# Adding u to the stored MLP output in DRAM, with accumulating transfers, in place of identity products on TensorE

## The chip, the cores and the metric

The kernel runs on one core of one Trainium2 chip. The metric is the device time of one execution in microseconds, as the median of several runs. A core has five engines with a queue of instructions each: TensorE (PE, with its weight loads as PEld), VectorE (DVE), ScalarE (ACT), GpSimd (POOL) and SyncE (SP), which issues most of the transfers. Transfers between DRAM and the on-chip memory run on 16 DMA engines.

## The reference

Causal block attention, then a token mix and an MLP with a residual, then a gated convolution:

```python
# attention: B=8, H=8, S=576, D=64; blocks of 64, block i sees blocks j <= i
attn = softmax(where(mask, q @ k^T / sqrt(D), -1e9));  x = attn @ v      # (8, 576, 512)
h = x^T @ U @ V                  # U 576x32, V 32x576, along the tokens
u = x + h^T
x = u + relu(u @ w_ch1) @ w_ch2  # 512 -> 2048 -> 512
gate = sigmoid(causal conv of 5 taps over the tokens, per channel)
out = (gate * (x @ w_val)) @ w_out
```

The change touches the `u +` of the MLP's output and nothing else of what is computed.

## The kernel before

Products run in float32r on operands split in a high and a low part (`hi_act`, L90, on ACT; `lo`, L96, on DVE or POOL), and each product is three: high by high, low by high, high by low. The 4608 tokens of all batches make 9 groups of 512 (`NG`, `GS`); features stand on partitions, so that a tile of u is 128 features by 512 tokens, and d counts the four feature blocks. The 2048 hidden features make 16 blocks f (`NF`), so the MLP runs in 144 steps s, step s being f = s mod 16 of group g = s // 16.

`mix_H` (L820) forms u: a product in PSUM, an add on DVE that leaves u in `xt` (L835), its high part `uh` on ACT (L836), its low part `ul` on POOL (L837). A batch has 576 tokens, so its u is cut in pieces for two groups or three, and pieces for a group too far ahead wait in the list `later` until the group two before has had its last hidden block (`y_done`).

`emit_h1(s)` makes a hidden block: 12 products (L963) into PSUM, relu to `hh` on ACT (L991), the low part `hl` on DVE (L992). `emit_o(s)` multiplies it with w2: 12 products (L1015) into four PSUM banks `acc`, one for each d, that collect over the 16 blocks of a group. `emit_o` runs one step behind `emit_h1`. At f = 0 it takes fresh banks, and the four d get eight products with an identity matrix `identr` first, one with `uh` and one with `ul` (L1008): this is how u comes into the sum. At f = 15 ACT copies the four banks to `y` (L1027) and SP writes each to DRAM, `y_s[g]` (L1028). From the first group to the seventh the pool of `y` has two buffers, so the third copy waits until the first write has landed and the fourth for the second.

Around a group boundary PE's order is: the w2 products of f = 15 of the old group, hidden blocks f = 0 and f = 1 of the new one, the identity products, the w2 products of f = 0. Boundary n below is the one at which group n begins, n from 0 to 8. Between the parts `gap` puts pieces of the attention of a later batch, a fixed pace of them for each group; attention ends during group 6, and group 7's part of u with it.

The order on PE is as the program is written. On the other engines the program's scheduler sets it, from a timeline that it estimates; instructions under `high_priority` go ahead. SP issues the loads of w2 (L951, 512 KB for each step), of q, k and v (L334, L345) and the writes of `y_s`, one after the other, and waits in its queue where a buffer isn't free. POOL does low parts, among them `vlo` of the attention (L97), which PE's pPV products use. The last stage reads `y_s` back (`load_y`, L1067): groups 0 and 1 during group 8, the rest after the MLP.

Of the kernel before, what the change touches and what calls it, by code (L numbers as in the profile page):

```python
# [8 lines left out]
F32 = mybir.dt.float32  # L9
F32R = mybir.dt.float32r  # L10
# [3 lines left out]
ALU = mybir.AluOpType  # L14
# [3 lines left out]
P = 128  # L18
# [4 lines left out]
def attn_moe_gate_kernel(ctx: ExitStack, tc: tile.TileContext, q, k, v, U, V, w1, w2, wval, convw, wout, out):  # L23
# [8 lines left out]
    ND = DM // P  # L32
    NF = DFF // P
    NP = H // 2
    GS = 512
    groups = [(t, min(GS, NT - t)) for t in range(0, NT, GS)]
    NG = len(groups)
# [41 lines left out]
    PAT = (0,1)  # L79
    URG = True  # L80
    UVAT = 14
    LOW = 2000
    NB32 = S // 32

# [3 lines left out]
    vec, act, pool, pe, sp = nc.vector, nc.scalar, nc.gpsimd, nc.tensor, nc.sync  # L88

    def hi_act(o, i):  # L90
        act.copy(o, i)  # L91
# [4 lines left out]
    def lo(eng, o, i, h):  # L96
        eng.tensor_tensor(o, i, f32(h), op=ALU.subtract)  # L97
# [50 lines left out]
    dram = ctx.enter_context(tc.tile_pool(name="dram", bufs=1, space=DRAM))  # L148
    const = ctx.enter_context(tc.tile_pool(name="const", bufs=1, side="left"))
# [13 lines left out]
    def open_mlp_psum():  # L163
        first.close()
        psum["acc"] = mlp.enter_context(tc.tile_pool(name="accp", bufs=1, space=PSUM, side="left"))
# [36 lines left out]
    ps_p = att.enter_context(tc.tile_pool(name="psp", bufs=ABUF, space=PSUM, side="right"))  # L202

    y_s = [dram.tile([P, ND, n], F32, name=f"y_s{g}") for g, (_, n) in enumerate(groups)]
    w2_s = [dram.tile([P, 2, DM], F32, name=f"w2_s{f}") for f in range(NF)]

    def ypos(t):
# [12 lines left out]
    ident = ac_p.tile([P, P], F32, name="ident")  # L220
# [6 lines left out]
        pool.memset(both[64 * a:64 * a + 64, 64 * a:64 * a + 64], 1.0)  # L227
    unit = const.tile([KC, KC], F32, name="unit")
    pool.tensor_copy(unit, ident[0:KC, 0:KC])
    identr = const.tile([P, P], F32R, name="identr")  # L230
    pool.tensor_copy(identr, ident)

    w1hi = w1_p.tile([P, ND, DFF], F32R, name="w1hi")
    w1lo = w1_p.tile([P, ND, DFF], F32R, name="w1lo")
# [26 lines left out]
    def setup_uv():  # L261
        ur = fetch(U, NTT * R, [(slice(0, n), slice(i * R, i * R + R), slice(t0, t0 + n), slice(0, R)) for i, (t0, n) in enumerate(tok)], True)
        ur = ur.rearrange("p (i r) -> p i r", r=R)
        for c in (0, 2, 3):
            (hi_act if UVE else hi_vec)(ust1[:, :, c * R:(c + 1) * R], ur)
        lo(vec, ust1[:, :, R:2 * R], ur, ust1[:, :, 0:R])
        for h in range(2):
            hs = slice(h * HS, (h + 1) * HS)
            vr = fetch(V, HS, [(slice(c * R, c * R + R), slice(0, HS), slice(0, R), hs) for c in range(4)])
            (hi_act if UVE else hi_vec)(vst[:, hs], vr)  # L270
            lo(vec, vst[3 * R:4 * R, hs], vr[3 * R:4 * R, :], vst[3 * R:4 * R, hs])
# [485 lines left out]
    ut = {}  # L757
    gst = {}

    def u_tiles(g):  # L760
        if g not in ut:
            ut[g] = [u_p.tile([P, ND, GS], F32R, tag="u" + x, name="u" + x) for x in "hl"]
        return ut[g]


    def mix_pieces(b):
        t0, t1 = b * S, (b + 1) * S
        r = []
        for g, (a, n) in enumerate(groups):
            lo_t, hi_t = max(a, t0), min(a + n, t1)  # L770
            if lo_t < hi_t:
                r.append((g, lo_t - t0, hi_t - t0, lo_t - a))
        return r
# [3 lines left out]
    def mix_H2(pn):  # L777
        mix_H(pn, 0)
        yield
        mix_H(pn, 1)  # L780
# [39 lines left out]
    def mix_H(pn, i):  # L820
        pcs = mix_pieces(pn // NP)
        if i >= len(pcs):
            return
        gi, a0, a1, off = pcs[i]
        if gi >= 2 and gi > y_done[0] + 2:
            later.append((pn, i))
            return
        xt = xts[pn]
        d = pn % NP
        uh, ul = u_tiles(gi)  # L830
        w = a1 - a0
        ps = ps_p.tile([P, 512], F32, tag="a", name="pH")
        pe.matmul(ps[:, 0:w], gst[pn], vst[:, a0:a1], start=True, stop=True)
        with tc.high_priority():
            vec.tensor_tensor(xt[:, a0:a1], ps[:, 0:w], xt[:, a0:a1], op=ALU.add)  # L835
        hi_act(uh[:, d, off:off + w], xt[:, a0:a1])  # L836
        lo(pool, ul[:, d, off:off + w], xt[:, a0:a1], uh[:, d, off:off + w])  # L837

# [116 lines left out]
    accs = {}  # L955
# [20 lines left out]
    def emit_h1(s, gap):  # L976
# [19 lines left out]
        gap()  # L996
        hts[s] = (hh, hl)

    def emit_o(s, gap):
        g, f = divmod(s, NF)  # L1000
        t0, n = groups[g]
        if f == 0:
            if g == 0:
                open_mlp_psum()
            accs[g] = [psum["acc"].tile([P, GS], F32, tag=f"acc{d}", name=f"acc{d}") for d in range(ND)]
            for d in range(ND):
                for i, u in enumerate(ut[g]):
                    pe.matmul(accs[g][d][:, 0:n], identr, u[:, d, 0:n], start=(i == 0), stop=False)  # L1008
        acc = accs[g]
        hh, hl = hts.pop(s)  # L1010
        w = w2t.pop(s)
        for d in range(ND):
            ds = slice(d * P, (d + 1) * P)
            for i, (wi, x) in enumerate(((0, hh), (0, hl), (1, hh))):
                pe.matmul(acc[d][:, 0:n], w[:, wi, ds], x[:, 0:n], start=False, stop=(f == NF - 1 and i == 2))  # L1015
            if d == 1:
                gap()
        gap()
        if f == NF - 1:
            ut.pop(g)  # L1020
            for d in range(ND):
                if pbp and g < NG - 1:
                    y = pbp["g"].tile([P, GS + HALO], F32, tag="gt", name="gt")
                else:
                    y = late["y"].tile([P, GS], F32, tag="y", name="y")
                with tc.high_priority():
                    act.copy(y[:, 0:n], acc[d][:, 0:n])  # L1027
                sp.dma_start(out=y_s[g][:, d, :], in_=y[:, 0:n])  # L1028
# [42 lines left out]
    def split_tiles(g, pb):  # L1071
        gate[g][1:3] = [pb.tile([P, ND, GS], F32R, tag="y" + x, name="y" + x) for x in "hl"]
# [19 lines left out]
    def val_begin(g, pg):  # L1092
        gated[g] = [pg.tile([P, ND, GS], F32R, tag="g" + x, name="g" + x) for x in "hl"]

    def emit_val(g, e, pg, pvs):
        t0, n = groups[g]
        y, yh, yl, gt, segs, wd = gate[g]
        gh, gl = gated[g]
        vh, vl = wv["v"]
        es = slice(e * P, (e + 1) * P)  # L1100
        ps = pvs.tile([P, GS], F32, tag="val", name="val")
        i = 0
        for d in range(ND):
            for w, x in ((vh, yh), (vh, yl), (vl, yh)):
                pe.matmul(ps[:, 0:n], w[:, d, es], x[:, d, 0:n], start=(i == 0), stop=(i == 3 * ND - 1))  # L1105
                i += 1
        gf = pg.tile([P, GS], F32, tag="gf", name="gf")
        for o, m, pp in segs:
            latest[0] = vec.tensor_tensor(gf[:, o:o + m], ps[:, o:o + m], gt[e][:, pp - HALO:pp - HALO + m], op=ALU.mult)
        hi_act(gh[:, e, 0:n], gf[:, 0:n])  # L1110
        lo(vec, gl[:, e, 0:n], gf[:, 0:n], gh[:, e, 0:n])
# [56 lines left out]
    for i, done in enumerate(stream):  # L1168
        if i == UVAT:
            setup_uv()  # L1170
# [14 lines left out]
    def gap():  # L1185
        tick_count[0] += 1
        if tick_count[0] % EVERY == 0:
            flush_later()
        pace[0] += pace[1]
        while pace[0] > 0 and pace[2] == 0:  # L1190
            pace[0] -= 1.0
            r = next(stream, 2)
            if r:
                pace[2] = r
                if r == 2:
                    while later:
                        flush_later()
                    open_pb()

    gated_conv[0] = GATE0  # L1200
    for s in range(NS + LAG):
        g, f = divmod(s, NF)
# [14 lines left out]
        if s < NS:  # L1217
# [11 lines left out]
            if g == NG - 1 and 4 <= f < 4 + 2 * ND:  # L1229
                g_, d = divmod(f - 4, ND)  # L1230
# [6 lines left out]
    with pb1:  # L1237
        with tc.tile_pool(name="pbs2", bufs=1, side="left") as pbs2, \
                tc.tile_pool(name="pbgd", bufs=2, side="left") as pbgd, \
                tc.tile_pool(name="pbo", bufs=3, side="left") as pbo, \  # L1240
                tc.tile_pool(name="pbpo", bufs=3, space=PSUM, side="left") as pbpo:
            pbs = (pbp["y1"], pbs2)
            pbps = pbp["ps"]
            for g in range(NG + 1):
                if g < NG:
                    val_begin(g, pbgd)
                    if g + 1 < NG:
                        split_tiles(g + 1, pbs[(g + 1) % 2])
                    for e in range(ND):
                        emit_val(g, e, pbgd, pbps)  # L1250
                        if g + 1 < NG:
                            split_y(g + 1, e)
                            if g > 0:
                                emit_gate(g + 1, e)
                    gate.pop(g)
                    if g + 2 < NG:
                        load_y(g + 2)
                if g > 0:
                    emit_out(g - 1, pbo, pbpo)
# [30 lines left out]
```

## Time and profile before

| | |
|---|---|
| time, median of 3 runs | 1433.97 us (1433.51 to 1435.35) |
| profiled execution: time, and its span | 1437.6 us, 1435.8 us |
| PE busy | 1392.8 us, 97% of the span |
| DVE busy | 1026.1 us, 71% |
| ACT busy | 698.5 us, 49% |
| POOL busy | 317.9 us, 22% |
| moved by the transfers | 163.58 MB |

The span is from the first to the last instruction that the profiler saw; the time has 1.8 us around it. Busy shares are averages over stages. Matmuls are pipelined: one is shown as 0.39 us long while the next starts 0.23 us after it, so the distance between starts is the price of one.

### The profile page before, as it was taken

Reading aid. Unit: us, or ns where it says so; the run is one execution under the profiler, and the core shown is the slowest. Engines: PE = TensorE matmul, PEld = TensorE weight load, DVE = VectorE, ACT = ScalarE, POOL = GpSimd, SP = SyncE. Lnnn points to the kernel's source line nnn. Section 1 sums busy time; section 2 is a strip of 40 time slices with the busy share of each in tenths; the row PEclk is TensorE's granted clock in tenths of the full one; section 3 lists DMA queues with packets and bytes.
Section 4 is the critical chain, followed back from the end, with each engine's and each line's share of the span. In section 5 each row is a group of like instructions: output and inputs, shape, how many; then the busy total and the mean of one; then the engine's idle time right before and its main releaser. Section 6 shows DMA issues by size and latency. Waiting matters only on the chain.

```text
span 1435.8 us, 20136 instructions
## 1 busy us (share of the span) xinstructions
PE 1392.8 (97%) x6762; PEld 1083.0 (75%) x6762; DVE 1026.1 (71%) x2105; ACT 698.5 (49%) x1539; POOL 317.9 (22%) x467
## 2 busy tenths in 40 slices
PE   6898978999999999999999999999999999999999
PEld 4666656777777777777777777778888888788887
DVE  5987889687777886888687787866225245499991
ACT  5775544555655555546455555555233211344342
POOL 3353441111121121112111211121032000344310
PEclk9999999999999999999999999999999999999999
DMA  6666775433343443434343333332255433223311
GB/s 110 155 156 202 226 235 140 114 84 97 90 113 84 93 106 103 98 87 125 84 99 88 110 88 99 84 97 83 87 177 170 151 104 131 75 83 101 110 52 66
DMA packets 246290, 163.58 MB, mean 114 GB/s; under 512 B 197669, under 2 KB 212261, under 8 KB 246186
## 3 DMA queue, kind: packets, MB, share of 16 engines
q1 hardware_dynamic: 243818, 161.99, 40.3%
q8 instruction: 54, 0.88, 0.3%
q10 hardware_dynamic: 2368, 0.30, 0.2%
q14 instruction: 50, 0.41, 0.1%
HBM read 134.98 MB, written 27.26 MB: 113 GB/s over the span
## 4 chain that ended last, share of the span: by engine, by line
PE 84%; DVE 6%; DMA 5%; ACT 3%; issue 1%; SPq 1%; POOL 0%; ACTq 0%; DVEq 0%; POOLq 0%
PE acc L1015 26%; PE h L963 25%; PE pPV L734 8%; PE o L1129 7%; PE val L1105 7%; PE pS L415 6%; DMA raw<-in_moe_w_ch_dram 3%; PE pG L810 1%; PE acc L1008 1%; PE pS L454 1%; DVE wa L125 1%; DVE wa L143 1%; DMA rawk<-in_k_dram 1%; PE pPV L542 1%; ACT s L469 1%
## 5 line engine op out<-in xcount | busy, mean ns | idle before, releaser
L1015 PE MATMUL acc<-hh,w 128*128 128x512 f32 x1152 | 401.5, 401 | 0.0
L1015 PEld LDWEIGHTS acc<-hh,w 128*128 128x128 f32 x1152 | 216.7, 188 | 65.4 <-issue 21.0
L963 PE MATMUL h<-uh,w1hi 128*128 128x512 f32 x576 | 237.1, 412 | 2.8 <-DVE xt L835 1.0
L963 PE MATMUL h<-uh,w1lo 128*128 128x512 f32 x576 | 226.5, 393 | 0.0
L963 PE MATMUL h<-ul,w1hi 128*128 128x512 f32 x576 | 226.0, 392 | 0.0
L1015 PE MATMUL acc<-hl,w 128*128 128x512 f32 x576 | 225.4, 391 | 0.0
L992 DVE SCALAR_TENSOR_TENSOR hl<-h,hh 128x512 fp32r<-128x512 f32 x144 | 98.5, 684 | 130.4 <-ACT hh L991 129.1
L991 ACT ACTIVATE hh<-h 128x512 fp32r<-128x512 f32 x144 | 85.8, 596 | 174.7 <-PE h L963 168.9
L963 PEld LDWEIGHTS h<-uh,w1hi 128*128 128x128 f32 x576 | 108.8, 189 | 46.6 <-issue 19.5
L97 POOL TENSOR_TENSOR vlo<-vstk,vhi 128x320 fp32r<-128x320 f32 x46 | 42.1, 916 | 457.0 <-ACT vhi L91 415.4
L963 PEld LDWEIGHTS h<-uh,w1lo 128*128 128x128 f32 x576 | 108.5, 188 | 24.2
L1015 PEld LDWEIGHTS acc<-hl,w 128*128 128x128 f32 x576 | 108.5, 188 | 19.5 <-issue 0.7
L963 PEld LDWEIGHTS h<-ul,w1hi 128*128 128x128 f32 x576 | 108.9, 189 | 18.7 <-issue 0.2
L1087 DVE SCALAR_TENSOR_TENSOR gt<-yb,cw,gt 128x516 f32<-128x516 f32 (+1 forms) x144 | 115.2, 831 | 1.4
L415 PE MATMUL pS<-tq,tk 64*128 64x320 f32 (+4 forms) x576 | 97.5, 427 | 5.0 <-ACT za L420 2.2
L97 POOL TENSOR_TENSOR yl<-yb,yh 128x512 fp32r<-128x512 f32 (+7 forms) x64 | 66.8, 1076 | 107.2 <-ACT yh L91 107.1
L420 ACT COPY s<-pS 128x320 f32<-128x320 f32 (+2 forms) x128 | 60.1, 497 | 52.3 <-PE pS L415 51.1
L97 POOL TENSOR_TENSOR ul<-xt,uh 128x512 fp32r<-128x512 f32 (+7 forms) x64 | 56.4, 888 | 93.4 <-ACT uh L91 93.2
L415 PEld LDWEIGHTS pS<-tq,tk 64*128 64x128 f32 x576 | 45.0, 185 | 41.9 <-issue 23.0
L670 ACT ACTIVATE s<-s 128x448 f32<-128x448 f32 (+1 forms) x62 | 43.8, 711 | 62.0 <-DVE s L646 61.8
L646 DVE TENSOR_TENSOR s<-s,mb 128x64 f32<-128x64 f32 (+4 forms) x160 | 67.3, 483 | 0.3
L97 DVE TENSOR_TENSOR el<-s,eh 128x448 fp32r<-128x448 f32 (+1 forms) x62 | 46.7, 787 | 17.6 <-PE pPV L734 9.8
(188 smaller groups left out, 2678.7 us busy)
## 6 DMA issues: line engine op xcount, KB each, us to landing
w<-w_s SPq DMA_DIRECT2D x144, 512.0 KB, 3.3
rawq<-in_q_dram SPq DMA_DIRECT2D x128, 72.0 KB, 2.9
out_dram<-ot SPq DMA_DIRECT2D x35, 256.0 KB, 2.0
rawk<-in_k_dram SPq DMA_DIRECT2D x124, 72.0 KB, 3.1
vstk<-in_v_dram SPq DMA_DIRECT2D x64, 128.0 KB, 2.6
raw<-in_moe_w_ch_dram SPq DMA_DIRECT2D x64, 128.0 KB, 2.8
raw<-in_moe_w_ch_dram SPq DMA_DIRECT2D x16, 512.0 KB, 3.9
w_s<-wo SPq DMA_DIRECT2D x16, 512.0 KB, 3.8
```

Source lines behind the costliest of these rows:

```text
L97: eng.tensor_tensor(o, i, f32(h), op=ALU.subtract)
L415: pe.matmul(t[:, o:o + w], tk[me, kslice(j)], tq[me, a0:a1], start=True, stop=True)
L420: act.copy(stt[n][half_of[j]][:, d:d + o], t[:, 0:o])
L646: noted(3, vec.tensor_tensor(sv(n, j), sv(n, j), mb[:, q0[j]:], op=ALU.subtract))
L734: pe.matmul(o_, l_, r_, start=(i == 0), stop=(i == len(todo) - 1))
L963: pe.matmul(ps[:, 0:n], w[:, d, fs], x[:, d, 0:n], start=(d == 0 and i == 0), stop=(d == ND - 1 and i == 2))
L991: act.activation(hh[:, 0:n], ps[:, 0:n], AF.Relu)
L992: latest[0] = vec.scalar_tensor_tensor(hl[:, 0:n], ps[:, 0:n], 0.0, f32(hh[:, 0:n]), op0=ALU.max, op1=ALU.subtract)
L1015: pe.matmul(acc[d][:, 0:n], w[:, wi, ds], x[:, 0:n], start=False, stop=(f == NF - 1 and i == 2))
L1087: vec.scalar_tensor_tensor(gt[d][:, 0:gw], y[:, d, j:j + gw], cw[:, d, j:j + 1], gt[d][:, 0:gw], op0=ALU.mult, op1=ALU.add)
L1105: pe.matmul(ps[:, 0:n], w[:, d, es], x[:, d, 0:n], start=(i == 0), stop=(i == 3 * ND - 1))
L1129: pe.matmul(ps[:m, cs], x[:, e, a:a + m], w[:, e, cs], start=(i == 0), stop=(i == 3 * ND - 1))
```

## The change

The identity matrix in float32r and the 72 identity products are gone (8 in each of 9 groups); the first w2 product of f = 0 now starts the bank (`start=True`). `mix_H` writes each finished piece of u to DRAM, to a new tile `u_s` in the layout of `y_s` (64 transfers on SP's queue, one for each piece). `add_u(g)` issues four transfers from POOL's queue, from DRAM to DRAM, that add `u_s[g]` to `y_s[g]` where it lies, 256 KB each. It stands in `emit_o` at f = 2 (`UAT`) of the group after; for the last group in the last stage, after the second `emit_val` of group 0.

```diff
@@ mix_H
         with tc.high_priority():
             vec.tensor_tensor(xt[:, a0:a1], ps[:, 0:w], xt[:, a0:a1], op=ALU.add)
+        sp.dma_start(out=u_s[gi][:, d, off:off + w], in_=xt[:, a0:a1])
         hi_act(uh[:, d, off:off + w], xt[:, a0:a1])
@@
+    def add_u(g):
+        for d in range(ND):
+            pool.dma_start(out=y_s[g][:, d, :], in_=u_s[g][:, d, :], accum_op=ALU.add)
+
     def emit_o(s, gap):
...
-            for d in range(ND):
-                for i, u in enumerate(ut[g]):
-                    pe.matmul(accs[g][d][:, 0:n], identr, u[:, d, 0:n], start=(i == 0), stop=False)
         acc = accs[g]
+        if f == UAT and g > 0:
+            add_u(g - 1)
...
-                pe.matmul(acc[d][:, 0:n], w[:, wi, ds], x[:, 0:n], start=False, stop=(f == NF - 1 and i == 2))
+                pe.matmul(acc[d][:, 0:n], w[:, wi, ds], x[:, 0:n], start=(f == 0 and i == 0), stop=(f == NF - 1 and i == 2))
@@ last stage
                         emit_val(g, e, pbgd, pbps)
+                        if g == 0 and e == 1:
+                            add_u(NG - 1)
```

On PE nothing but the 72 products leaves the order. On SP's queue, at boundary 3, before (y_s_115 is the output of group 2, `rawq` and `rawk` are raw tiles of q and k, `w` is a w2 tile):

```order
L951 DMA w_5585<-w_s_137 128x1024
L334 DMA rawq<-in_q_dram 32x18x32 x2
L334 DMA rawk<-in_k_dram 32x18x32 x2
L334 DMA rawq<-in_q_dram 32x18x32 x2
L334 DMA rawk<-in_k_dram 32x18x32 x2
L951 DMA w_5706<-w_s_122 128x1024
L1028 DMA y_s_115<-y 128x512 x2
L951 DMA w_5739<-w_s_123 128x1024
L1028 DMA y_s_115<-y 128x512 x2
```

And now (u_s_125 and u_s_126 belong to groups 3 and 4):

```order
L836 DMA u_s_125<-xt 128x320
L334 DMA rawq<-in_q_dram 32x18x32
L836 DMA u_s_126<-xt 128x256 x2
L334 DMA rawq<-in_q_dram 32x18x32
L836 DMA u_s_126<-xt 128x256
L334 DMA rawk<-in_k_dram 32x18x32
L952 DMA w_5729<-w_s_131 128x1024
L334 DMA rawk<-in_k_dram 32x18x32
L1032 DMA y_s_115<-y 128x512 x2
L836 DMA u_s_126<-xt 128x256
L952 DMA w_5762<-w_s_132 128x1024
L1032 DMA y_s_115<-y 128x512
```

Four pieces of u now stand ahead of the first two writes of `y_s`, and one more ahead of the other two. On ACT's queue at the same place, before (the four copies out of the banks with a high part of u between them; `xt`, `lt`, `eh` and `ef` are attention work):

```order
L1027 COPY y<-acc_4367 128x512
L1027 COPY y<-acc_4368 128x512
L91 CAST uh<-xt 128x256
L1027 COPY y<-acc_4369 128x512
L1027 COPY y<-acc_4370 128x512
L735 COPY xt<-pPV 64x128
L736 COPY lt<-pPV 64x128
L91 CAST eh<-s_5162 128x448
L91 CAST eh<-s_5163 128x768
```

And now:

```order
L1031 COPY y<-acc_4386 128x512
L1031 COPY y<-acc_4387 128x512
L92 CAST uh<-xt 128x256
L1031 COPY y<-acc_4388 128x512
L735 COPY xt<-pPV 64x128
L736 COPY lt<-pPV 64x128
L92 CAST eh<-s_5179 128x448
L1031 COPY y<-acc_4389 128x512
L92 CAST eh<-s_5180 128x768
```

The fourth copy has moved three places back; the third, which waits for the first write of `y_s`, stands where it stood. On POOL's queue the four accumulating transfers stand around a low part of v, here those of boundary 3 as they are now:

```order
L98 TENSOR_TENSOR ul<-xt,uh 128x256 x4
L1002 DMA y_s_115<-u_s_124 128x512 x3
L98 TENSOR_TENSOR vlo<-vstk_166,vhi 128x320
L1002 DMA y_s_115<-u_s_124 128x512
L98 TENSOR_TENSOR vlo<-vstk_165,vhi 128x320
```

Three of the four stand ahead of the first `vlo`; before, no transfer stood on this queue at this place.

## Rows read from the trace of the kernel before

**Rows 1.** Busy time by stretch: window and length in us, then each engine (instructions)

```profile
113.00:263.00 150.00, 131.68 (x633) 96.35 (x630) 124.99 (x241) 75.07 (x164) 48.11 (x54) 0.98 0.64 192
263.00:1149.00 886.00, 883.92 (x4293) 689.90 (x4292) 615.79 (x1357) 449.51 (x941) 157.58 (x265) 1.00 0.39 105
```

**Rows 2.** Instructions of L1008: count, shortest, median, longest ns, first and last start

```profile
L1008 PE MATMUL acc<-uh,identr x36: 387/389/499, 113.3 to 1149.4; 128*128 128x512 f32 x36
```

**Rows 3.** PE in order of time at boundary 3: start us, length us, instruction

```profile
547.24 0.39 PE L1008 MATMUL acc<-uh,identr 128*128 128x512 f32 x1
...
549.06 0.39 PE L1015 MATMUL acc<-hh,w 128*128 128x512 f32 x1
```

**Rows 4.** ACT and DVE in order of time at boundary 3

```profile
541.47 1.07 ACT L1027 COPY y<-acc 128x512 f32<-128x512 f32 x2 [3.00 <-DMA y_s<-y]
...
547.27 0.60 ACT L991 ACTIVATE hh<-h 128x512 fp32r<-128x512 f32 x1
...
547.90 0.69 DVE L992 SCALAR_TENSOR_TENSOR hl<-h,hh 128x512 fp32r<-128x512 f32 x1
```

**Rows 5.** First identity product and hl of f=0, boundaries 1, 2, 4, 5, 6, 7

```profile
276.33 0.47 PE L1008 MATMUL acc<-uh,identr 128*128 128x512 f32 x1
272.16 0.69 DVE L992 SCALAR_TENSOR_TENSOR hl<-h,hh 128x512 fp32r<-128x512 f32 x1 [1.99 <-ACT hh L991]
413.60 0.40 PE L1008 MATMUL acc<-uh,identr 128*128 128x512 f32 x1
413.04 0.69 DVE L992 SCALAR_TENSOR_TENSOR hl<-h,hh 128x512 fp32r<-128x512 f32 x1
680.68 0.39 PE L1008 MATMUL acc<-uh,identr 128*128 128x512 f32 x1
681.43 0.65 DVE L992 SCALAR_TENSOR_TENSOR hl<-h,hh 128x512 fp32r<-128x512 f32 x1
813.64 0.39 PE L1008 MATMUL acc<-uh,identr 128*128 128x512 f32 x1
814.61 0.65 DVE L992 SCALAR_TENSOR_TENSOR hl<-h,hh 128x512 fp32r<-128x512 f32 x1
946.73 0.39 PE L1008 MATMUL acc<-uh,identr 128*128 128x512 f32 x1
948.18 0.65 DVE L992 SCALAR_TENSOR_TENSOR hl<-h,hh 128x512 fp32r<-128x512 f32 x1
1058.64 0.39 PE L1008 MATMUL acc<-uh,identr 128*128 128x512 f32 x1
1058.22 0.69 DVE L992 SCALAR_TENSOR_TENSOR hl<-h,hh 128x512 fp32r<-128x512 f32 x1 [2.81 <-ACT hh L991]
```

**Rows 6.** SP's queue at boundary 3: writes of y_s, two and two

```profile
537.03 1.01 SPq L1028 DMA_DIRECT2D y_s<-y  x2
542.08 1.71 SPq L1028 DMA_DIRECT2D y_s<-y  x2
```

**Rows 7.** Stretches before and during that write: last two columns DMA share, GB/s

```profile
532.00:537.00 5.00, 5.00 (x25) 4.16 (x24) 4.48 (x11) 2.77 (x6) 3.17 (x4) 1.00 0.78 122
537.00:541.50 4.50, 4.50 (x25) 3.81 (x24) 4.25 (x14) 1.03 (x4) 0.80 (x1) 1.00 0.94 298
```

**Rows 8.** POOL's vlo after boundary 3, and the first product that uses it

```profile
546.12 0.89 POOL L97 TENSOR_TENSOR vlo<-vstk,vhi 128x320 fp32r<-128x320 f32 x1 [6.77 <-DMA vstk<-in_v_dram]
...
556.91 0.37 PE L734 MATMUL pPV<-eh,vlo 128*64 128x448 f32 x1
```

**Rows 9.** A w2 load in group 8, its first product, and all such loads (KB, us to landing)

```profile
1152.78 0.32 SPq L951 DMA_DIRECT2D w<-w_s  x1
...
1160.75 0.39 PE L1015 MATMUL acc<-hh,w 128*128 128x512 f32 x1
...
w<-w_s SPq DMA_DIRECT2D x144, 512.0 KB, 3.3
```

More of the change, by code (lines that the diff above doesn't have):

```diff
@@ L81, in attn_moe_gate_kernel @@
     UVAT = 14
+    UAT = 2
     LOW = 2000
@@ L204, in attn_moe_gate_kernel @@
     y_s = [dram.tile([P, ND, n], F32, name=f"y_s{g}") for g, (_, n) in enumerate(groups)]
+    u_s = [dram.tile([P, ND, n], F32, name=f"u_s{g}") for g, (_, n) in enumerate(groups)]
     w2_s = [dram.tile([P, 2, DM], F32, name=f"w2_s{f}") for f in range(NF)]
@@ L229, in attn_moe_gate_kernel @@
     pool.tensor_copy(unit, ident[0:KC, 0:KC])
-    identr = const.tile([P, P], F32R, name="identr")
-    pool.tensor_copy(identr, ident)
     w1hi = w1_p.tile([P, ND, DFF], F32R, name="w1hi")
```

## The prediction

> **What bounds the kernel now.** I read the busy time by stretch first, since a share over the whole span mixes stages. From 263 to 1149 us PE is busy 883.92 of 886 us at the full granted clock, and no other engine comes near that [rows 1]: eight of the nine group boundaries lie there, and a product that leaves PE should come off the end, unless PE then waits. From 113 to 263 us PE is busy only 131.68 of 150 us [rows 1], and boundary 0 lies there (the identity products start at 113.3 [rows 2]). Next I read PE in order of time at a boundary, for the price of the block: its eight products take from 547.24 to the first w2 product at 549.06, so 1.82 us [rows 3]. The 0.39 us that each row shows overlap, and eight of them would come out at 3.1 us, which is wrong. Last I looked at what the block hides. After it come `acc<-hh` and `acc<-hl` of f = 0, and these need `hh` and `hl`, which ACT and DVE make from a hidden block that PE finished a little before. Without the block `acc<-hh` would stand where the block starts and `acc<-hl` 0.23 us behind. At boundary 3 the block starts at 547.24, `hh` is only begun at 547.27, and `hl` ends at 547.90 + 0.69 = 548.59 [rows 4]. So the block is cover there, not only cost.
>
> **What it removes.** Eight blocks of 1.82 us lie in the bound stretch: 14.6 us. The ninth, at boundary 0, lies where PE waits for others; it is worth between 0 and 1.8 us, and I take 0, because 18 of 150 us are idle there. From the 14.6 us comes off what PE now waits for `hl`, that is the end of `hl` less the start of the block plus 0.23 us:
> - boundary 1: `hl` ends at 272.85, needed at 276.56: no wait, gain 1.82 [rows 5].
> - boundary 2: 413.73 against 413.83: no wait, gain 1.82 [rows 5].
> - boundary 3: 548.59 against 547.47: wait 1.12, gain 0.70 [rows 3, 4].
> - boundary 4: 682.08 against 680.91: wait 1.17, gain 0.65 [rows 5].
> - boundary 5: 815.26 against 813.87: wait 1.39, gain 0.43 [rows 5].
> - boundary 6: 948.83 against 946.96: wait 1.87, more than the block, gain 0 [rows 5].
> - boundary 7: 1058.91 against 1058.87: wait 0.04, gain 1.78 [rows 5].
> - boundary 8: no attention is left beside it, so I take it like boundary 1, gain 1.82 (an estimate).
>
> The sum is 9.0 us, if `hh` and `hl` come when they come now.
>
> **What it adds on SP.** They won't come quite when they do now. At boundary 3 ACT stands 3.00 us idle before the third copy out of the banks, until the first write of `y_s` has landed [rows 4]; that write was issued at 537.03 [rows 6], so it took 4.44 us to 541.47. Behind the copy in ACT's queue stand the attention's copies and casts and then `hh`, without a gap up to 547.27 [rows 4]. A write that lands later by some time moves `hh`, `hl` and PE's wait by as much. The new SP queue has four pieces of u ahead of that write; the first belongs to an earlier step, the other three are 128 by 256 values, 3 × 131,072 bytes = 0.39 MB. Nothing in the trace shows such a write, so I bound the delay. From below: nothing, since the pieces are issued among the q and k loads some microseconds earlier, when the engines are 0.78 busy, not full [rows 7]. A gain is excluded, since nothing leaves the queue. From above, by bytes at the 298 GB/s that the stretch of the write moves [rows 7]: 0.39 MB / 298 GB/s = 1.3 us. The pieces grow by 64 tokens a boundary (320, 384, 448), which gives 1.65, 2.0 and 2.3 us at boundaries 4, 5 and 6; at 2 and 7, with smaller or fewer pieces ahead, I put 0.4 each (an estimate). Boundaries 1 and 8 have over 3 us to spare or no attention to delay. The upper sum is 8.1 us. I take the half, 4.0 us: part of the pieces has landed by then, and the engines are nearly full (0.94) while the write is under way, so the rest does push it back. No work is added on DVE or ACT.
>
> [...]
>
> **What it adds on POOL and the DMA engines.** Four accumulating transfers in each of nine groups: 36 × 256 KB, read twice and written once. They are off PE's path unless they hold up one of two things. First, POOL's own queue: three of them stand ahead of a `vlo`, and the third waits until the third write of `y_s` has landed. That write is issued at about 542.1 [rows 6], so it lands near 546.5 at 4.44 us. `vlo` then starts near 547 in place of 546.12, plus the issue of one transfer, takes 0.89 us, and is used at 556.91 [rows 8]: some 9 us to spare. Behind it stand one more transfer, another `vlo` and memsets. The issue itself is not in the trace: SP's takes about 0.5 us each (1.01 us for two [rows 6]); POOL's would have to take 9 us before PE sees it. I take 0. Second, the w2 loads: in group 8, where they are closest, one is issued at 1152.78 and first used at 1160.75, 7.97 us later, and takes 3.3 us to land [rows 9]. It may be slower by a factor of 2.4 at no cost. The accumulating transfers move 1 MB in a group that lasts over 90 us; I take 0, and up to 4 us in all if a load or two in each of the eight groups is late by 0.25 us. The read of `y_s` in the last stage waits for adds that are long done, but for the last group's, which has most of the last stage to land: 0.
>
> **Sum.** −9.0 + 4.0 = −5.0 us. The profiled execution of 1437.6 us becomes 1432.6 us. It stands 3.6 us above the median of 1433.97 us; the difference is a shift of the whole and belongs to no step, so the same change from the median gives 1429.0 us.
>
> **Rivals.** *The whole block is kept:* PE doesn't wait, because the attention's work settles itself a little later and `hl` comes first, or the waits at boundaries 3 to 6 are paid back by PE running ahead less. Against it: the program's order on PE is fixed, and `hl` ends 1.1 to 1.9 us too late there. It would give 14.6 us: 1419.4 us.
>
> *The bytes all stand in the way:* the delay is the upper sum of 8.1 us, and nearly all that is won goes: −9.0 + 8.1 = −0.9, 1433.1 us. For it: the engines are 0.94 busy while the write is under way [rows 7].
>
> *The pieces move slower than the large transfers, and the kernel gets slower:* a piece has rows of 1 KB. In the stretch from 532 to 537 us, with q and k loads of small rows, the engines were 0.78 busy at 122 GB/s, so 156 GB/s would fill them [rows 7]. At that rate the three pieces are 2.5 us at boundary 3, then 3.1, 3.8 and 4.4, with 0.8 each at 2 and 7: 15.4 us, and the time is 1434.0 − 9.0 + 15.4 = 1440.4 us. It decides for slower by 0.2% from a delay of 9.0 + 2.9 = 11.9 us, that is if three quarters of the pieces are still under way when the write is issued. Against it: SP issues them up to 5 us ahead.
>
> *POOL is held by its issues:* an issue of several us would push `vlo` out. The rows show no such transfer, and there is 9 us to spare; at 10 us for the third one PE would wait about 1 us at five boundaries, at 12 us about 3 us: 1434 to 1444 us. Beside it stands the Trainium skill, "SBUF — State Buffer", sections "SBUF: two separate sides" and "A bandwidth-pool intuition that's wrong (but worth ruling out)": GpSimd writes the descriptors of its transfers itself and is locked out while certain DVE operations hold the port they share, with 3.1 us measured in place of 0.62. By that figure the third transfer is still inside the 9 us; no run here shows it.
>
> **How the numbers follow.** The forecast, with a delay between a third and three quarters of the upper sum (1427.7 to 1431), has 0.43. The whole block has 0.12, all bytes in the way 0.20, slow pieces 0.13, POOL or late w2 loads 0.12, of which 0.07 end within 0.2% and 0.05 beyond. A measurement of this kernel tells about 0.2%, 2.9 us, from no change. Faster: 0.43 + 0.12 = 0.55. Within: 0.20 + 0.07 = 0.27. Slower: 0.13 + 0.05 = 0.18. The range runs from the whole block, 1419 us, to 1438 us, part of the way into the slow pieces, and leaves out some 0.15 beyond its upper end.
>
> **What would show it.** PE should lack 72 products and from boundary 3 to 6 have a new idle time of 1 to 2.5 us before `acc<-hl` of f = 0, put down to DVE `hl`; at boundaries 1, 2 and 8 none. ACT's wait for `DMA y_s<-y` at boundary 3 should grow from 3.00 us to about 3.7. If it stays at 3.0, the delay is nothing and the gain 9 us; if it passes 5 us, the slow pieces are true. A wait of PE on POOL `vlo`, or of `acc` on a w2 load, would prove me wrong on the third part.

## The result and the profile after

The changed kernel takes 1454.12 us (median of 4 runs, 1452.92 to 1457.0) beside 1434.66 us of the kernel before in the same comparison: 1.0133 of it, with a 95% interval of 1.012 to 1.0146. It is slower by about 19 us. The forecast was 1429.0 us, in a range up to 1438.

The page of the changed kernel's profile shows the busy time of the engines, then two DMA queues with packets, MB and share of the 16 DMA engines over the span (q0 holds POOL's transfers, q1 almost all others), then two kinds of transfer with KB each and median us to landing:

```profile
PE 1386.7 (96%) x6690; PEld 1075.0 (74%) x6690; DVE 1019.1 (70%) x2105; ACT 700.7 (48%) x1539; POOL 345.5 (24%) x502
...
q1 hardware_dynamic: 253034, 171.43, 42.2%
q0 software_dynamic: 5184, 9.44, 5.0%
...
w<-w_s SPq DMA_DIRECT2D x144, 512.0 KB, 3.3
...
y_s<-u_s POOLq DMA_DIRECT2D x36, 256.0 KB, 7.3
```

PE has 72 products less and its work is smaller, as the diff says, and yet the span is 1451.1 us. In the stretches that answer to [rows 1]:

```profile
113.00:263.00 150.00, 130.60 (x627) 96.80 (x624) 117.13 (x240) 76.50 (x163) 49.17 (x54) 0.94 0.66 200
263.00:1149.00 886.00, 866.60 (x4190) 671.83 (x4188) 612.60 (x1355) 445.61 (x935) 179.92 (x293) 1.00 0.48 119
```

From 263 to 1149 us PE was busy 883.92 of 886 us; now it is 866.60. So 19.4 us stand idle in the stretch where 2.1 us did before. The list of what PE waits for (waited for, us in total, times, longest) has these two next to each other, behind one of 8.7 us at the start of the span that the kernel before has too:

```profile
PE acc L1019 <- DMA w<-w_s: 7.9, 2, 6.8
PE pT L802 <- ACT lt L736: 6.6, 5, 1.5
```

To see where the time goes, I took the start of each PE instruction in a profile less the start of the same instruction in the profile of the kernel before (the order on PE is the same but for the 72 products). The table gives it in us at four times of the kernel before, positive where PE is later, for all kernels that follow; "end" is the difference of the spans, and the last column is the timed ratio with its interval.

| kernel | 263 | 1055 | 1075 | 1165 | end | ratio |
|---|---|---|---|---|---|---|
| changed | 1.8 | 5.6 | 12.5 | 12.1 | 15.3 | 1.0133 (1.012 to 1.0146) |
| e1, no adds | −0.5 | 0.4 | 0.5 | −1.3 | −1.3 | 1.0011 (0.9995 to 1.0027) |
| e2, no u at all | 0.5 | −4.1 | −5.0 | −6.8 | −6.6 | 0.9967 (0.9954 to 0.9981) |
| e3, adds under f = 8 | 0.0 | 4.4 | 10.7 | 13.0 | 16.4 | 1.0118 (1.0096 to 1.014) |
| e4, u from ACT's queue | 2.3 | 1.8 | 6.7 | 6.9 | 10.5 | 1.0076 (1.0051 to 1.0101) |
| e5, adds held | 3.5 | 5.2 | 3.9 | 2.3 | 4.8 | 1.0064 (1.0045 to 1.0083) |
| e6, all adds held, u from ACT | 4.4 | 3.9 | 2.1 | 0.6 | 1.0 | 1.0002 (0.9992 to 1.0011) |
| e8, adds and u held | −0.1 | −3.9 | −5.7 | −6.6 | −6.5 | 0.998 (0.9969 to 0.9991) |
| e10, e8 with group 0's block | 0.4 | −3.7 | −5.5 | −7.1 | −6.8 | 0.9969 (0.9957 to 0.9981) |
| e11, only group 0's block gone | 0.1 | −1.0 | −0.2 | −0.2 | 0.0 | 1.0016 (1.0004 to 1.0027) |
| e7, DVE adds in groups 7, 8 | −0.4 | −0.3 | −2.1 | −3.9 | −3.9 | 0.9976 (0.9964 to 0.9987) |
| e9, mixture | 0.1 | −0.5 | −2.3 | −4.1 | −4.1 | 0.9971 (0.9961 to 0.9982) |

A profile is one execution: that of the kernel before is about 3 us above its median, others are up to 2.7 us off theirs, and the column "end" lies between 4.4 us below and 0.7 us above what the ratios say. The changed kernel loses in three places: slowly up to 1055 us, 7 us at once in group 7, and 3 us in the last stage.

### The profile page after: what moved, and what is told of

It reads as the page before. It is cut to its first block, busy times and chain, and to the rows that moved or that the text cites. A ratio compares the mean times of both kernels' runs of the same rounds, so it can differ in the third digit from the quotient of the medians.

```text
span 1451.1 us, 20187 instructions
## 1 busy us (share of the span) xinstructions
PE 1386.7 (96%) x6690; PEld 1075.0 (74%) x6690; DVE 1019.1 (70%) x2105; ACT 700.7 (48%) x1539; POOL 345.5 (24%) x502
## 3 DMA queue, kind: packets, MB, share of 16 engines
q1 hardware_dynamic: 253034, 171.43, 42.2%
q0 software_dynamic: 5184, 9.44, 5.0%
## 4 chain that ended last, share of the span: by engine, by line
PE 79%; DMA 7%; DVE 6%; ACT 4%; issue 1%; SPq 1%; ACTq 0%; POOL 0%; DVEq 0%
PE acc L1019 25%; PE h L964 23%; PE pPV L734 7%; PE o L1133 7%; PE val L1109 7%; PE pS L415 5%; DMA raw<-in_moe_w_ch_dram 3%; DMA y_s<-y 2%; DMA w<-w_s 1%; PE pS L454 1%; PE pG L810 1%; PE pPV L542 1%; DVE wa L126 1%; DVE wa L144 1%; ACT s L469 1%
## 5 line engine op out<-in xcount | busy, mean ns | idle before, releaser
L1019 PE MATMUL acc<-hh,w 128*128 128x512 f32 x1152 | 406.2, 405 | 10.0 <-DMA w<-w_s 7.9
```

What stands on the lines that cost most here:

```text
L1019: pe.matmul(acc[d][:, 0:n], w[:, wi, ds], x[:, 0:n], start=(f == 0 and i == 0), stop=(f == NF - 1 and i == 2))
```

## Which part costs: the adds, the writes of u, or the removal

Theory A put most of the loss on the accumulating transfers, theory B on the writes of u, theory C on a new order in group 0. The first experiment leaves out the adds:

```diff
     def add_u(g):
-        for d in range(ND):
-            pool.dma_start(out=y_s[g][:, d, :], in_=u_s[g][:, d, :], accum_op=ALU.add)
+        return
```

> The changed kernel without the 36 accumulating transfers; u is still written to DRAM, and the output lacks the residual u. Theory A, the accumulating transfers cost most of the loss (they fill the DMA engines after a boundary, so that the write of u and with it a w2 load land late in group 7): the 7.0 us wait of acc on the w2 load at 1082 us of the changed kernel's trace is gone, and the time is about 1431 us. Theory B, the writes of u on SP's queue cost most (the third copy out of the banks, hh and hl late at boundaries 3 to 6): the time stays at 1445 us or above. Theory C, the other order in group 0 costs most: about 1450.

The second leaves out the writes as well:

```diff
-        sp.dma_start(out=u_s[gi][:, d, off:off + w], in_=xt[:, a0:a1])
```

> The changed kernel without the accumulating transfers and without the writes of u, so with nothing but the removal of the identity products; the output lacks the residual u. This is the size of the removal by itself. By the sum of the prediction without a delay, 9.0 us are won: 1425.7 us beside 1434.7 of the kernel before. If the block had covered nothing, 14.6: 1420. If PE loses the time elsewhere, at once or later in the group, 1434. Theory A expects it to be some 4 us below the kernel that still writes u, theory B some 20 us below it.

Measured: 1.0011 and 0.9967. In steps of the ratios, times 1434.7 us: the removal by itself gains 4.7 us, the writes of u give back 6.3, and the adds cost 17.5; by the intervals each of these is known to 2 or 3 us. Theory A holds for the greater part, but B isn't nothing: without the adds the kernel would have come out even.

The waits at boundary 3 show B at work. PE in order of time with nothing of u (e2):

```profile
544.29 0.51 PE L1017 MATMUL acc<-hh,w 128*128 128x512 f32 x1 [0.43 <-ACT hh L991]
545.37 0.50 PE L1017 MATMUL acc<-hl,w 128*128 128x512 f32 x1 [0.57 <-DVE hl L992]
```

PE waits 0.43 and 0.57 us there, 1.0 us in sum; the prediction had 1.12 from [rows 3, 4]. With the writes of u (e1), PE waits for ACT ahead of that too, and again at the w2 products, and ACT waits 3.86 us for the first write of `y_s` in place of 3.00 [rows 4]. First PE's rows, then ACT's, and under them ACT's row of the changed kernel, with the adds:

```profile
543.94 0.30 PE L802 MATMUL pT<-ident,xt 128*64 128x128 f32 x1 [1.02 <-ACT lt L736]
...
546.14 0.49 PE L1018 MATMUL acc<-hh,w 128*128 128x512 f32 x1 [0.51 <-ACT hh L992]
546.87 0.50 PE L1018 MATMUL acc<-hl,w 128*128 128x512 f32 x1 [0.23 <-DVE hl L993]
```

```profile
539.68 0.59 ACT L1030 COPY y<-acc 128x512 f32<-128x512 f32 x1 [3.86 <-DMA y_s<-y]
```

```profile
543.93 0.59 ACT L1031 COPY y<-acc 128x512 f32<-128x512 f32 x1 [4.03 <-DMA y_s<-y]
```

From 263 us to the end e2 gains 7.1 us and e1 0.8: 6.3 us for the writes, between the 4.0 that the prediction took and the 8.1 at which it put all bytes in the way.

## When the adds leave, and what they collide with

The next two kernels move a part each. In e3 one number changes:

```diff
-    UAT = 2
+    UAT = 8
```

> The changed kernel with one number changed: the accumulating transfers are issued at f = 8 of the next group and not at f = 2. Theory A in the form that they collide with what SP does right after a boundary: the 7 us wait in group 7 goes and the delay of the v loads and w2 loads there with it, about 1446 us. Theory A in the form that their mere load on the engines costs wherever it falls: 1452 to 1456. Theory B: 1454, no change.

In e4 the writes of u are issued by ACT, behind the cast:

```diff
-        sp.dma_start(out=u_s[gi][:, d, off:off + w], in_=xt[:, a0:a1])
         hi_act(uh[:, d, off:off + w], xt[:, a0:a1])
+        act.dma_start(out=u_s[gi][:, d, off:off + w], in_=xt[:, a0:a1])
```

> The changed kernel with the writes of u issued from ACT's queue, behind the cast of the same piece, in place of SP's. Theory B in the form that they stand ahead of the writes of y_s in SP's queue: ACT waits for the first write of y_s at boundary 3 as long as in the kernel before, 3.0 us, and the time falls by 4 to 6 us. In the form that their bytes are in the way on the engines: no change there, and the issues on ACT, 64 by some 0.5 us, cost something: 1454 to 1458. Theory A: 1454.

e3 came out at 1.0118: no change. Its trace says why. The adds of boundary 3 in the changed kernel, POOL in order of time:

```profile
544.33 1.67 POOL L1002 DMA_DIRECT2D y_s<-u_s  x2 [3.56 <-DMA y_s<-y]
547.37 0.81 POOL L1002 DMA_DIRECT2D y_s<-u_s  x1 [1.37 <-PE h L964]
548.58 0.89 POOL L98 TENSOR_TENSOR vlo<-vstk,vhi 128x320 fp32r<-128x320 f32 x1 [0.39 <-ACT vhi L92]
554.32 0.80 POOL L1002 DMA_DIRECT2D y_s<-u_s  x1 [4.86 <-DMA y_s<-y]
```

And in e3:

```profile
544.63 1.67 POOL L1002 DMA_DIRECT2D y_s<-u_s  x2 [4.22 <-DMA y_s<-y]
547.71 0.81 POOL L1002 DMA_DIRECT2D y_s<-u_s  x1 [1.41 <-DMA y_s<-y]
```

The scheduler put the adds at the same places of POOL's order in both kernels: all 36 leave within 2 us of each other, each once its own write of `y_s` has landed, and the first two in the middle of the boundary, while the third and fourth writes are still to come. Moving the statement moved nothing.

e4 took 1.0076, 8 us less than the changed kernel. In the profile the gain is 4.3 us from 263 to 1055 us and 2 us in group 7, where the w2 load is still late (PE waits 5.0 us for it); to the end only 4.8 us are left, and with four runs the ratio is known to 3.6 us either way. How long the first write of `y_s` takes, from its issue to the third copy, speaks for both forms of theory B: at boundary 3 it is 5.10 us beside 5.18 in the changed kernel and 4.44 in the kernel before, which fits bytes that are in the way from any queue; at boundary 6 it is 3.41 beside 5.61 and 3.15, which fits a place in SP's queue. In e1, without the adds, it is 5.11 at boundary 3 and 5.49 at boundary 6, so the adds have no part in the delay of that write.

In e5 the adds of the first eight groups are held by a dependency on `hl` of f = 9, the latest hidden block that exists where they are written:

```diff
+            i = pool.dma_start(out=y_s[g][:, d, :], in_=u_s[g][:, d, :], accum_op=ALU.add)
+            if g < NG - 1:
+                tc.add_manual_dep(i.ins, latest[0].ins.name, ...)
-    UAT = 2
+    UAT = 8
```

> The changed kernel with the accumulating transfers of the first eight groups held back until hl of the hidden block f = 9 of the next group exists, by an added dependency; before, they left as soon as the four writes of y_s had landed, at the boundary, whatever f they were written under. Theory A1, they cost by colliding with the writes of y_s, the u write that frees a buffer and the w2 load at a boundary: the 6.9 us wait on the w2 load in group 7 falls to 1 or 2 us, the landing of y_s goes back from 5.1 us to 3.4 us in the median, and the time is 1443 to 1446 us (3 us stay in the last stage, whose transfers are not held). Theory A2, their load on the DMA engines costs wherever it falls: 1450 or above.

Measured 1.0064: half of the loss is gone with the same 36 adds. A write of `y_s` lands after 3.6 us in the median, where it took 5.1 in the changed kernel and 3.3 in the kernel before. The adds of boundary 3 now leave 76 us later:

```profile
619.91 3.34 POOL L1002 DMA_DIRECT2D y_s<-u_s  x4 [7.90 <-DVE r L634]
```

In the table the 6.9 us between 1055 and 1075 have turned into a gain of 1.3. What happened there in the changed kernel is on SP's queue:

```profile
1062.76 0.39 SPq L836 DMA_DIRECT2D u_s<-xt  x1
1070.87 0.34 SPq L252 DMA_DIRECT2D raw<-in_moe_conv_w_dram  x1
1071.26 0.35 SPq L1045 DMA_DIRECT2D raw<-in_moe_w_val_dram  x1
1071.79 0.59 SPq L1071 DMA_DIRECT2D yb<-y_s  x1
1072.43 0.71 SPq L952 DMA_DIRECT2D w<-w_s  x1
```

The last write of u is issued at 1062.76. The load of the convolution's weights (L252) takes over the memory of the attention's tiles and so must wait until that write has read its tile; it waits 7.6 us in SP's queue (the list of what SP waits for):

```profile
SPq L252 <- DMA u_s<-xt: 7.6, 1, 7.6
```

Behind it stands the w2 load of step f = 2, which leaves at 1072.43, and PE waits for it:

```profile
1082.08 0.77 PE L1019 MATMUL acc<-hh,w 128*128 128x512 f32 x1 [6.85 <-DMA w<-w_s]
```

The wait costs more than its length. While PE stands idle the granted clock (the column ahead of the last two) falls to 0.50, the lower of its two levels, 1.2 GHz, and the products that follow start 0.43 us apart in place of 0.23 until it is back at the upper one, 2.4 GHz, at about 1085.6:

```profile
1080.00:1082.00 2.00, 0.00 (x0) 0.00 (x0) 0.30 (x1) 1.26 (x3) 1.62 (x2) 0.50 0.59 210
1082.00:1084.00 2.00, 1.92 (x5) 1.58 (x6) 0.56 (x1) 1.41 (x3) 2.00 (x2) 0.50 0.94 363
```

PE falls back by 8.7 us in group 7, 6.85 for the wait and 1.9 for the slow products; the table's 6.9 is that less the 1.8 us of the missing block.

In e5 the same queue goes on after 2.5 us, and PE's wait at that product is 0.23 us:

```profile
1062.52 0.38 SPq L836 DMA_DIRECT2D u_s<-xt  x1
1065.43 0.34 SPq L252 DMA_DIRECT2D raw<-in_moe_conv_w_dram  x1
...
1066.99 0.62 SPq L952 DMA_DIRECT2D w<-w_s  x1
```

Two adds left just ahead of that write of u, at 1061.18 and 1062.11, and the other two at 1067.35 and 1068.64. The first row below is the stretch in which the write of u was under way, the second the one behind it, with the last two adds on their way (last two columns: share of the DMA engines, GB/s):

```profile
1062.70:1070.87 8.17, 8.17 (x38) 6.77 (x37) 1.38 (x2) 1.23 (x3) 3.16 (x4) 1.00 0.96 181
1070.00:1075.00 5.00, 5.00 (x24) 3.99 (x22) 0.00 (x0) 0.00 (x0) 0.12 (x1) 1.00 0.97 91
```

The engines are 0.96 busy at 181 GB/s and then 0.97 busy at 91. In the kernel before, 0.94 busy went with 298 GB/s [rows 7]. Over the whole execution q0 moves 9.44 MB in 5.0% of the 16 engines' span of 1451.1 us, 130 GB/s while busy, and q1 171.43 MB in 42.2%, 280 GB/s: per byte, an accumulating transfer holds the engines for about twice as long as the others.

## The last stage, and the writes of u held as well

e6 holds the last group's adds until group 3 of the last stage (shown against e5) and issues u from ACT, as e4 does:

```diff
-            if g < NG - 1:
-                tc.add_manual_dep(i.ins, latest[0].ins.name, ...)
+            tc.add_manual_dep(i.ins, latest[0].ins.name, ...)
-                        if g == 0 and e == 1:
+                        if g == 3 and e == 1:
                             add_u(NG - 1)
```

> As the one above, and the writes of u are issued from ACT's queue behind the cast, and the last group's four transfers are held until after the second val of group 3 of the last stage. Theory A1 and B together: the 3.3 us that the last stage loses between 1240 and 1260 us go as well, since POOL's yl casts no longer stand behind a transfer that waits; the time is 1434 to 1438 us, no gain over the kernel before, because the writes of u still cost some 4 to 7 us that eat the removal. If the writes of u on ACT cost nothing: 1430.

Measured 1.0002: no loss and no gain. The 3.3 us between 1165 us and the end of the changed kernel are gone (0.5 in e6). In the changed kernel POOL waits there with an add at the head of its queue, and its eight `yl` casts start some 0.9 us later against PE's order; a DVE instruction of 0.48 us then takes 3.98 us, until POOL is through (POOL, then DVE):

```profile
1255.37 0.81 POOL L1002 DMA_DIRECT2D y_s<-u_s  x1 [5.86 <-DMA y_s<-y]
1255.91 5.88 POOL L98 TENSOR_TENSOR yl<-yb,yh 128x128 fp32r<-128x128 f32 x8
```

```profile
1258.11 3.98 DVE L1089 TENSOR_SCALAR gt<-yb,cw 128x516 f32<-128x516 f32 x1
1262.00 0.68 DVE L98 TENSOR_TENSOR gl<-gf,gh 128x512 fp32r<-128x512 f32 x1
```

PE waits for DVE there, 2.43 us in place of 0.79 (the changed kernel, then the kernel before), and loses about as much again with the products that follow at the lower clock (0.71 granted from 1265.4 to 1268 us, 0.53 to 1270):

```profile
1265.43 0.47 PE L1109 MATMUL val<-yh,wvh 128*128 128x512 f32 x1 [2.43 <-DVE gf L1113]
```

```profile
1251.74 0.47 PE L1105 MATMUL val<-yh,wvh 128*128 128x512 f32 x1 [0.79 <-DVE gf L1109]
```

The same DVE instruction in e6, and POOL's eight casts there:

```profile
1247.00 0.48 DVE L1090 TENSOR_SCALAR gt<-yb,cw 128x516 f32<-128x516 f32 x1
```

```profile
1243.90 6.75 POOL L98 TENSOR_TENSOR yl<-yb,yh 128x128 fp32r<-128x128 f32 x8 [9.95 <-ACT yh L92]
```

That POOL's casts hold the DVE instruction in the changed kernel is read from the two ends, 1261.79 and 1262.09, and was not tried apart. In e6 the same instruction stands in the middle of the same eight casts and is done in 0.48 us, so a row of casts beside it is not enough; what else it takes is open.

e8 is e6 with u on SP's queue again, and the pieces formed around a boundary (`hold_u`, from f = 15 of a group to f = 1 of the next) kept back until `hl` of f = 2 exists:

```diff
+        if hold_u[0]:
+            held.append((u_s[gi][:, d, off:off + w], xt[:, a0:a1]))
+        else:
+            sp.dma_start(out=u_s[gi][:, d, off:off + w], in_=xt[:, a0:a1])
...
+        if f == 1 and hold_u[0]:
+            hold_u[0] = False
+            while held:
+                o, x = held.pop(0)
+                i = sp.dma_start(out=o, in_=x)
+                tc.add_manual_dep(i.ins, latest[0].ins.name, ...)
```

> The changed kernel with all three collisions taken away: the accumulating transfers held to f = 9 of the next group, the last group's to group 3 of the last stage, and the pieces of u that are formed around a boundary written on SP's queue only after hl of f = 2 of the new group, behind the writes of y_s. If it was their places and not their work that cost, the boundaries gain what they gained with no u at all: 7 us from 263 us to the end in the profile, and a time at 0.9967 of the kernel before, 1430 us. If the 64 writes cost by their work, wherever they stand: 1436, as with u on ACT's queue.

The profile does what was expected: from 300 us on its lead is that of e2, which has no u at all, within 0.8 us. ACT's wait for the first write of `y_s` at boundary 3 is below the 3.00 us of before [rows 4], and PE's waits there are those of e2. ACT, then PE:

```profile
538.39 1.08 ACT L1044 COPY y<-acc 128x512 f32<-128x512 f32 x2 [2.69 <-DMA y_s<-y]
```

```profile
544.86 0.49 PE L1026 MATMUL acc<-hh,w 128*128 128x512 f32 x1 [0.51 <-ACT hh L997]
545.84 0.51 PE L1026 MATMUL acc<-hl,w 128*128 128x512 f32 x1 [0.48 <-DVE hl L998]
```

So by the profile the 64 writes and 36 adds cost PE almost nothing when they stand away from the boundaries. The time is 0.998 of the kernel before, 2.9 us faster, where 0.9967 was expected; the two intervals overlap, so by the times the transfers cost 1.9 us, and nothing or 4 us are as possible.

## Group 0

The changed kernel, e1, e5 and e8 came out 3 to 4 us short of their profiles, and e7 and e9, which keep group 0's block, did not; so the block was suspected. e11 takes that block alone out of the kernel before, and e10 gives it back to e8 (group 0 then writes and adds nothing in DRAM):

```diff
-            for d in range(ND):
+            for d in range(ND if g > 0 else 0):
                 for i, u in enumerate(ut[g]):
                     pe.matmul(accs[g][d][:, 0:n], identr, u[:, d, 0:n], start=(i == 0), stop=False)
```

> The kernel before without the identity products of group 0 alone, so the output lacks u in group 0; nothing is added. The prediction put the block of group 0 at 0 to 1.8 us of gain: 1433 to 1435 us. If the other order in group 0 costs 2 to 4 us: 1437 to 1439 us, 1.002 of the kernel before.

> As the version with the writes of u held, but group 0 keeps its identity products and sends nothing through DRAM. That version's profile gained 6.4 us from 263 us to the end and its time only 2.9 us; all kernels without group 0's block fall 2 to 4 us short of their profiles in this way, and the two that keep it do not. If taking group 0's block (and with it the order that the scheduler gives the other engines before 263 us) loses those 2 to 4 us: 0.9955 of the kernel before, about 1429 us. If the shortfall has another cause: 0.998 as there, 1432.

e11 is 1.0016 (1.0004 to 1.0027) of the kernel before: taking out eight products makes it 2.3 us slower. The interval is 0.6 to 3.9 us. The scheduler then gives DVE, ACT and POOL another order of weight conversions and attention work in group 0. In the kernel before, three stretches of 50 us from 113 us read (the column ahead of the last two is the granted clock):

```profile
113.00:163.00 50.00, 43.92 (x228) 32.34 (x225) 39.66 (x72) 26.91 (x66) 17.99 (x17) 1.00 0.74 226
163.00:213.00 50.00, 41.39 (x212) 29.77 (x211) 41.44 (x68) 25.14 (x53) 20.75 (x22) 0.97 0.71 222
213.00:263.00 50.00, 46.36 (x196) 34.24 (x195) 43.89 (x103) 23.01 (x47) 9.37 (x17) 0.97 0.49 129
```

And in e11:

```profile
113.00:163.00 50.00, 44.64 (x241) 33.67 (x240) 33.93 (x72) 28.55 (x71) 18.38 (x19) 0.98 0.73 223
163.00:213.00 50.00, 44.21 (x222) 32.99 (x221) 35.38 (x64) 25.31 (x51) 22.08 (x22) 0.91 0.66 212
213.00:263.00 50.00, 45.12 (x181) 32.23 (x181) 46.65 (x108) 24.10 (x47) 9.76 (x17) 0.90 0.53 149
```

More of PE's work is done in the first two (x241 and x222 beside x228 and x212), less in the third, and the granted clock is 0.91 and 0.90 in place of 0.97: for a larger part of these stretches PE ran at the lower of its levels, 1.2 GHz, and for the rest at 2.4. In this one profile the two kernels are level again by 263 us, while the times differ by 2.3 us; a profile is one execution, and which of the waits in group 0 makes the difference in the others is open. e10 is 0.9969, 1.6 us better than e8; the two intervals overlap, so this fits e11 but doesn't add to it. Nor does the suspicion hold as a rule: e3, e4 and e6 lack the block too and are within 1 us of their profiles, and e10, which keeps it, is 2.4 us short of its own. The shortfalls follow from how far each profiled execution lies from the median of its kernel, and say nothing of the block.

## Two versions without all the transfers

e7 adds no transfer. It drops the block in groups 7 and 8 alone, where no attention runs, and adds u on DVE as the banks are copied out (`EV` is 7):

```diff
-                    act.copy(y[:, 0:n], acc[d][:, 0:n])
+                    if g < EV:
+                        act.copy(y[:, 0:n], acc[d][:, 0:n])
+                    else:
+                        vec.tensor_tensor(y[:, 0:n], acc[d][:, 0:n], f32(u[0][:, d, 0:n]), op=ALU.add)
+                        vec.tensor_tensor(y[:, 0:n], y[:, 0:n], f32(u[1][:, d, 0:n]), op=ALU.add)
```

> The kernel before, and in groups 7 and 8 alone the identity products are gone; there u is added as the banks are copied out, by two adds on DVE for each d (acc + uh, then + ul) in place of ACT's copy. No transfer is added. At boundaries 7 and 8 the removal was worth 1.8 us each in the trace without u, less 1.0 us by the w2 load of group 7 that then lands late: 1434.5 - 2.6 = 1431.9 us. If eight DVE adds at boundary 8 and in the last stage are in the way: 1434 or above. If the w2 load takes all of boundary 7's gain: 1432.7.

Measured 0.9976, 3.4 us faster; the profile gains 1.8 us at each of the two boundaries (the table, 1055 to 1075 and on to 1165) and keeps them. The expectation took 1.0 us off for a late w2 load in group 7, and that was wrong in its reason too: what e2 loses there is a wait for `hh`, which stands on ACT behind four casts of `yb` that wait for their load. ACT, in e2:

```profile
1063.02 2.18 ACT L92 CAST yh<-yb 128x512 fp32r<-128x512 f32 x4 [6.00 <-DMA yb<-y_s]
1065.11 1.07 ACT L991 ACTIVATE hh<-h 128x512 fp32r<-128x512 f32 x2
```

e9 adds groups 1 and 2 to that, with u through DRAM and the adds held to f = 9, and keeps the block in group 0 and in groups 3 to 6:

```diff
+    EV = 7
+    UD = (1, 2)
+        if gi in UD:
+            sp.dma_start(out=u_s[gi][:, d, off:off + w], in_=xt[:, a0:a1])
```

> A mixture of what was seen to gain: identity products kept in groups 0 and 3 to 6, where they cover the wait for hl; in groups 1 and 2 u goes through DRAM with the four transfers held to f = 9; in groups 7 and 8 u is added on DVE as the banks are copied out. Four boundaries gain 1.8 us each: 1436.1 - 7.2 = 1428.9 us, 0.995 of the kernel before. If the writes of u of groups 1 and 2 cost in group 0 what they seemed to cost with u on ACT's queue (up to 4 us by 263 us): 1432, no better than with DVE's adds alone.

Measured 0.9971, not to be told from e7: boundaries 1 and 2 gave 1.8 us each at the block's place, and PE lost most of it around them (1.6 us ahead of the block at boundary 1, 0.7 us after it, 0.8 us ahead of the one at boundary 2). The lead of 0.5 us at 1055 us is all that was left. Holding the writes of u there too, as e8 does, was not tried in this mixture. e7, e9 and e10 are 3 to 4 us faster than the kernel before, and the measurement doesn't rank them; e7 is the simplest.

## Why the prediction was wrong

**What bounds the kernel, and the price of the block** were right. e2 gains 1.8 to 1.9 us at boundaries 1, 2, 7 and 8, 0.6 and 0.35 at 3 and 4, nothing at 5 and 6, against 1.82, 0.70, 0.65, 0.43 and 0 as forecast; 1.0 us of it is lost again in group 7, where `hh` stands behind ACT's casts of `yb`. That makes 7.1 us from 263 us on where the sum said 9.0. The rival in which the whole block is kept fell.

**Boundary 0 at nothing** was off by a small loss: 2.3 us in e11, with an interval of 0.6 to 3.9. The prediction looked only at whether PE would gain there, not at the other order that three engines get when eight products leave.

**The delay by the writes of u** was the right mechanism, mis-sized: 6.3 us where 4.0 were taken and 8.1 was the upper sum; it lies about half way between the forecast and the rival with all bytes in the way. PE pays for it at another product than forecast: once u is written it waits mainly for `lt`, an attention copy behind the third copy on ACT (6.6 us in 5 waits in the changed kernel), and for `hl` only 0.9 us, where 1 to 2.5 us at each of four boundaries were named.

**The accumulating transfers at 0** is the step that failed, and it turned the sign: 17.5 us. The time at which they leave was about right: at boundary 3 the prediction let the third add wait for the third write of `y_s`, which it put near 546.5 us, and that add left at 547.37. What it made of this failed in two ways. It spread their 1 MB over the 90 us of a group, where the four leave within some 10 us of a boundary, take 7.3 us to land, and keep the engines 0.96 busy at 181 GB/s just when writes of `y_s` and u are under way. And it compared the w2 load's own flight with its slack, factor 2.4, but not what stands ahead of that load in SP's queue: in group 7 the load was issued 7 us later than in the kernel before, behind an instruction that waited for a write of u. The rival on POOL and late w2 loads named the w2 loads, at 4 us in all; its part on POOL looked at `vlo`, which never held PE, and no issue on POOL took more than 1.12 us.

In the table, the changed kernel less e1, the adds cost 2.9 us from 263 to 1055 us, 6.8 in group 7, 1.4 in group 8 and 3.2 in the last stage, 14.3 in all. The other 2.3 us stand at 263 us already, before the first add leaves at 269.24, and e3, with the same adds, is level there; so they are not shown to be the adds'.

**The last stage at 0** missed 3.3 us: not the read of `y_s`, which the prediction considered, but a late DVE instruction, beside POOL's casts behind a waiting add; e6, which holds that add, is without the loss.

By the ratios, −4.7 + 6.3 + 17.5 = 19.1 us, which is the measured loss by construction, since these are steps from kernel to kernel. The signs listed at the end of the prediction served: ACT's wait at boundary 3 grew to 4.03 us, where 3.7 was forecast, and the wait of `acc` on a w2 load, named as the one that would prove the third part wrong, is the largest of PE's waits from 263 us on.

## What to carry to other kernels

A transfer that replaces work on the bound engine has a place and a time of its own: find out when it can leave, not where it is written, and what stands behind it in its queue and behind whatever waits for it. The same 100 transfers cost 24 us at the group boundaries and about 2 us, not clear of nothing, when the adds left 30 to 80 us later and the writes of u around a boundary up to 20 us later. And work that covers a wait is worth less than its length, so cost its removal boundary by boundary, as held here to 2 us in 9.

## What the runs showed of the hardware

A 256 KB accumulating transfer from DRAM to DRAM landed after 7.3 us in the median, and while two were under way the DMA engines were 0.97 busy at 91 GB/s. After 6.85 us without a product PE's granted clock was 0.50, and products started 0.43 us apart in place of 0.23 until 3.5 us later. POOL's issue of one took 0.81 us (four in a row 3.34 us), beside 0.44 us in the median for a write of u on SP. A DVE instruction of 0.48 us took 3.98 us beside a row of eight POOL casts; here the Trainium skill, "SBUF — State Buffer", section "SBUF: two separate sides", says that a GpSimd operation and certain operations of DVE share a port pair, which the one that starts first holds for its whole instruction. The row agrees in that DVE went on within 0.3 us of POOL's last cast; it goes further in that several casts passed while DVE waited, and in e6 the same instruction took 0.48 us among the same casts.
